# Transposing q and k of a lightning-attention block on VectorE instead of TensorE

## The chip, the cores and the metric

The kernel runs on one core of one Trainium2 chip. The metric is the device time of one execution in microseconds (us). A profiled execution gives the span from the first to the last instruction and what each engine did in it. Engines are named as in the profile: PE is TensorE, PEld its weight loads, DVE is VectorE, ACT is ScalarE, POOL is GpSimd and SP is SyncE, which only issues transfers here.

## The reference

Two blocks, one behind the other. The first is lightning attention with a decay per head, over B, H, S, D = 4, 8, 768, 64:

```python
for b in range(nb):                       # blocks of 64 positions
    intra = einsum('bhic,bhjc->bhij', qb, kb) * Dmask
    intra = einsum('bhij,bhjd->bhid', intra, vb)
    inter = einsum('bhid,bhde->bhie', qb * lam_pow, kv_state)
    out[:, :, sl] = intra + inter
    kv_state = lam_block * kv_state + einsum('bhsd,bhse->bhde', kb * rev_pow, vb)
```

Its output, laid out as x of 3072 tokens by 512 features, goes through `h = x @ w_in; g = h - tanh(h); out = g @ w_out`, with w_in 512 x 2048 and w_out 2048 x 512. Everything is float32 at the output; the weights arrive as 64-bit floats and are rounded on the chip.

## The kernel before, in words

The sequence is cut into NG = 6 groups of BLK = 128 positions. A group holds one **chunk** per batch element b, so there are 24 chunks (g, b), each with all 8 heads; heads go in NP = 4 pairs, since two heads of 64 features fill 128 partitions. One group of 4 chunks gives 512 tokens, one pass of the dense block.

`load` (L116) issues three transfers a chunk on SP's queue, one each for q, k and v. Each puts 128 positions on the partitions and 8 heads x 64 features behind them (256 KB in packets of 256 bytes). Their buffers come from rings: 2 for q, 3 for k, 4 for v. A load waits until the last reader of its buffer is done, and the loads behind it on the queue wait with it.

`att_transpose` (L227) needs q and k with features on the partitions. PE transposes each pair of heads (L234) into a PSUM bank, `tq` or `tk`; ACT copies the banks to `qt` and `kt` in SBUF (L237, L238; two buffers each); DVE makes `qd`, q times the powers of the decay, from `tq` (L242, not in the first group), and multiplies `k_nat` in place by the decay to the end of the block (L245, not in the last group). `att_scores` (L248) multiplies `kt` by `qt` on PE and masks on DVE (L259). `att_out` joins the masked scores times v with `qd` times the running state (L296, L302); ACT brings the result to SBUF as `xt` (L306). `att_state` forms k times v (L271) and adds it to the state on DVE (L275, L276). `att_sums` forms sums of blocks of x (L312 to L315).

The dense block of the first group is plain (`up_plain` L437, `down_plain` L454) while weights arrive and are rounded. From the second group on both products are done with seven block products in place of eight (`up` L366, `down` L408): an up stage for each of four u, then a down stage, with products in the order 1, 2, 6, 5, 7, 4, 3. They use PSUM banks y (two), z and w (one each), which ACT and DVE clear (L342 to L355, L376, L377, L383, L384, L412, L414). The weights of the down products, `wb`, 1 MB each, are loaded on POOL's queue into two buffers (L395).

Attention of group g+1 is woven into the dense block of group g by hand, in pieces: the first two chunks' transposes after u=1, their scores after u=2, their output and state after down product 2; the other two chunks' transposes after product 6, their scores after 5, and the rest after 7:

```python
for n, more in ((2, p0[2:]), (6, p1[0:1]), (5, p1[1:2]), (7, p1[2:])):
    down(g, n)
    run(more)
```

Beyond that, the order on each engine and all waits are set by the framework when the kernel is built.

Of the kernel before, what the change touches and what calls it, by code (L numbers as in the profile page):

```python
# [9 lines left out]
F32 = mybir.dt.float32  # L10
# [3 lines left out]
AF = mybir.ActivationFunctionType  # L14
AL = mybir.AluOpType

BLK = 128
# [5 lines left out]
def kernel(  # L23
# [31 lines left out]
    nc = tc.nc  # L55
    B, H, S, D = q.shape
    NTOK, DM = out.shape
    DFF = moe_w_in.shape[1]
    NP = H // 2
    KI = DM // 128  # L60
    KO = DFF // 128
    NG = S // BLK
# [10 lines left out]
    io = ctx.enter_context(tc.tile_pool(name="io", bufs=4))  # L73
# [9 lines left out]
    ident = const.tile([128, 128], F32)  # L83
# [5 lines left out]
    for j in range(2):  # L89
        for p in range(NP):  # L90
            h = 2 * p + j
# [3 lines left out]
    fwd = const.tile([128, NP, BLK], F32)  # L95
# [16 lines left out]
    raw = {}  # L112
# [2 lines left out]

    def load(n):  # L116

        while at["loaded"] < min(n, len(chunks)):
            g, b = chunks[at["loaded"]]
            t = []  # L120
            for name, src, bufs in (("q", q, 2), ("k", k, 3), ("v", v, 4)):
                x = io.tile([128, H, D], F32, name=f"{name}_nat", tag=name, bufs=bufs)
                nc.sync.dma_start(out=x, in_=src[b, :, ts(g, BLK), :].rearrange("h s d -> s h d"))
                t.append(x)
            raw[g, b] = t
            at["loaded"] += 1

# [66 lines left out]
    def round_block(w, raw64):  # L194
# [18 lines left out]
        nc.vector.tensor_tensor(wi, wi, r, op=AL.add)  # L213

    load(2)
    load_weights(WAHEAD)

# [3 lines left out]
    def bank(name, tag, bufs):  # L221
        return psum.tile([128, 512], F32, name=name, tag=tag, bufs=bufs)


    tr, sc, kdec, xt = {}, {}, {}, {}

    def att_transpose(g, bs):  # L227
        for b in bs:
            load(g * B + b + 1)
            qn, kn, _ = raw[g, b]  # L230
            tq, tk = (bank(n, "att", 4).rearrange("d (p s) -> d p s", p=NP) for n in ("tq", "tk"))
            for t, x in ((tq, qn), (tk, kn)):
                for p in range(NP):
                    nc.tensor.transpose(out=t[:, p, :], in_=x[:, 2 * p:2 * p + 2, :], identity=ident)  # L234
            qt = work.tile([128, NP, BLK], F32, name="qt", tag="qt")
            kt = work.tile([128, NP, BLK], F32, name="kt", tag="kt")
            nc.scalar.activation(qt, tq, AF.Copy)  # L237
            nc.scalar.activation(kt, tk, AF.Copy)  # L238
            qd = None
            if g > 0:  # L240
                qd = work.tile([128, NP, BLK], F32, name="qd", tag="qd")
                nc.vector.tensor_tensor(qd, tq, fwd, op=AL.mult)  # L242
            if g < NG - 1:
                kp = kn.rearrange("s (p j) d -> s p j d", j=2)
                nc.vector.tensor_tensor(kp, kp, bwd, op=AL.mult)  # L245
            tr[g, b] = (qt, kt, qd)

# [14 lines left out]
    def att_state(g, bs):  # L262
        if g == NG - 1:
            return

        kv = bank("kv", "att", 4).rearrange("d (b p e) -> d b p e", b=2, p=NP)
        for n, b in enumerate(bs):
            _, kd, vn = raw[g, b]
            for p in range(NP):
                for j in range(2):  # L270
                    nc.tensor.matmul(out=kv[ts(j, 64), n, p, :], lhsT=kd[:, 2 * p + j, :], rhs=vn[:, 2 * p + j, :],  # L271
                                     start=n == 0 and p == 0, stop=True, skip_group_check=True)
        st = state[:, bs[0]:bs[0] + 2]
        if g > 0:
            nc.vector.tensor_tensor(st, st, lam_blk, op=AL.mult)  # L275
            nc.vector.tensor_tensor(st, st, kv, op=AL.add)  # L276
        else:
            nc.vector.tensor_copy(st, kv)

    def att_out(g, bs):  # L280
        half = bs[0] // 2
        xt[g, half] = xpool.tile([128, KI, HB], F32, name=f"xt{half}", tag=f"xt{half}")

        ops = [bank("op", "att", 4).rearrange("d (p b s) -> d p b s", p=2, b=2) for _ in range(2)]

        def dst(n, p, j):
            return ops[p // 2][ts(j if p < 2 else 1 - j, 64), p % 2, n, :]


        if g > 0:  # L290
            for n, b in enumerate(bs):
                for p in (0, 1):
                    for j in range(2):
                        r = ts(j, 64)
                        for pp in (p, p + 2):
                            nc.tensor.matmul(out=dst(n, pp, j), lhsT=state[r, b, pp, :], rhs=tr[g, b][2][r, pp, :],  # L296
                                             start=n == 0 and p == 0, stop=False, skip_group_check=True)
        for n, b in enumerate(bs):
            ss, vn = sc.pop((g, b)), raw[g, b][2]
            for p in range(NP):  # L300
                for j in range(2):
                    nc.tensor.matmul(out=dst(n, p, j), lhsT=vn[:, 2 * p + j, :], rhs=ss[:, j, p, :],  # L302
                                     start=g == 0 and n == 0 and p % 2 == 0, stop=n == 1 and p % 2 == 1,
                                     skip_group_check=True)
        for x in range(2):
            nc.scalar.activation(xt[g, half][:, 2 * x:2 * x + 2, :].rearrange("d p (b s) -> d p b s", b=2), ops[x], AF.Copy)  # L306
# [11 lines left out]
    def attention(g):  # L318
        pieces = [[(fn, g, bs) for fn in (att_transpose, att_scores, att_out, att_state)] for bs in ((0, 1), (2, 3))]
        pieces[1].append((att_sums, g, None))  # L320
        return pieces
# [234 lines left out]
```

## Time and profile before

| what | value |
|---|---|
| median of 3 runs | 723.77 us (722.71 to 724.51) |
| the profiled execution, whole | 722.81 us |
| its span | 721.0 us |
| granted TensorE clock | 0.988 |
| PE busy | 698.4 us (97%) |
| DVE busy | 337.4 us (47%) |
| ACT busy | 182.5 us (25%) |
| SP's queue q1 | 76,000 packets, 20.98 MB |
| chain that ended last, on PE | 89% of the span |

Busy time is the time in which at least one instruction of that engine ran. The chain is followed back from the last instruction to whatever released each step. A row of the groups of instructions names line, engine, operation, output and inputs, and gives busy time, mean duration and the idle time in front. The profiled execution took 1.8 us more than its span and 1.0 us less than the median of the runs.

### The profile page before, as it was taken

The page shows a single profiled execution, that of the slowest core. Times are in us where ns is not written, and L with a number is a line of the kernel's source. Part 1 is how long each engine was busy: PE and PEld are TensorE (multiplying, and loading weights), DVE is VectorE, ACT ScalarE, POOL GpSimd, SP SyncE. Part 2 cuts the span into 40 slices and gives each one's busy share as a digit, 9 for nine tenths or more (in the row PEclk, how much of TensorE's full clock was granted, in tenths as well). Part 3 has the DMA queues.
Part 4 walks back from the last instruction along what each step waited for, and adds up shares of the span by engine and source line. Part 5 has one row for each costly group of instructions (what it writes and reads, how often), then busy time and mean ns, then how long its engine had stood idle before and what let it go on. Part 6 is the DMA issues. An engine that isn't in the chain of part 4 may idle for free.

```text
span 721.0 us, 9989 instructions
## 1 busy us (share of the span) xinstructions
PE 698.4 (97%) x4224; PEld 585.4 (81%) x4224; DVE 337.4 (47%) x575; ACT 182.5 (25%) x312; POOL 68.1 (9%) x115
## 2 busy tenths in 40 slices
PE   6789999999999999999999999999999999999996
PEld 5568865557888888888888888888888888888885
DVE  6778956862656131564422455422345522254400
ACT  3536413423421210332200342111242111132100
POOL 0222202311000001000101000001000101100110
PEclk9799999999999999999999999999999999999998
DMA  9997708855101755011556110556310332400341
GB/s 212 237 217 222 250 3 262 266 163 170 29 1 62 216 178 159 1 30 58 160 160 171 65 30 5 167 166 172 106 45 0 113 116 93 147 1 0 132 143 76
DMA packets 89324, 86.63 MB, mean 120 GB/s; under 512 B 76864, under 2 KB 76864, under 8 KB 84800
## 3 DMA queue, kind: packets, MB, share of 16 engines
q0 software_dynamic: 13136, 65.02, 27.1%
q1 hardware_dynamic: 76000, 20.98, 14.1%
q8 instruction: 33, 0.54, 0.3%
q14 instruction: 11, 0.09, 0.0%
q10 hardware_dynamic: 144, 0.00, 0.0%
HBM read 72.36 MB, written 13.63 MB: 119 GB/s over the span
## 4 chain that ended last, share of the span: by engine, by line
PE 89%; DVE 4%; DMA 3%; ACT 2%; issue 2%; SPq 1%; POOLq 0%; POOL 0%; ACTq 0%
PE y L408 19%; PE y L366 18%; PE z L366 9%; PE z L408 9%; PE op L454 8%; PE h L437 7%; PE w L408 5%; PE w L366 4%; PE op L302 3%; DMA raw<-in_moe_w_in_dram 2%; PE sp L255 2%; DVE ss L259 2%; PE tk L234 1%; PE op L296 1%; PE tq L234 1%
## 5 line engine op out<-in xcount | busy, mean ns | idle before, releaser
L408 PE MATMUL y<-wb,g 128*128 128x256 f32 x640 | 142.3, 380 | 0.7 <-ACT o L349 0.7
L408 PEld LDWEIGHTS y<-wb,g 128*128 128x128 f32 x640 | 120.9, 190 | 18.0 <-ACT o L349 1.1
L366 PE MATMUL y<-xt,w 128*128 128x256 f32 x320 | 74.0, 382 | 1.1 <-ACT g L347 1.1
L376 ACT ACTIVATE th<-g 128x512 f32<-128x512 f32 x60 | 37.8, 630 | 141.7 <-DVE g L344 96.8
L366 PEld LDWEIGHTS y<-xt,w 128*128 128x128 f32 x320 | 60.1, 190 | 11.3 <-ACT g L347 2.7
L437 PE MATMUL h<-xt,w 128*128 128x256 f32 x256 | 61.9, 401 | 6.9 <-DVE w L213 4.7
L395 POOL DMA_DIRECT2D wb<-factors x35 | 18.9, 540 | 493.7 <-PE y L408 383.2
L437 PEld LDWEIGHTS h<-xt,w 128*128 128x128 f32 x256 | 50.6, 202 | 15.2 <-issue 3.5
L377 DVE TENSOR_TENSOR g<-g,th 128x512 f32<-128x512 f32 x60 | 41.4, 691 | 35.5 <-ACT th L376 35.5
L454 PE MATMUL op<-wt,g 128*128 128x512 f32 x128 | 56.1, 595 | 0.0
L454 PEld LDWEIGHTS op<-wt,g 128*128 128x128 f32 x128 | 24.0, 190 | 28.5 <-issue 27.7
L259 DVE TENSOR_TENSOR ss<-sp,mask 128x512 f32<-128x512 f32 x48 | 30.8, 682 | 27.3 <-PE sp L255 27.3
L350 DVE TENSOR_TENSOR g<-g,z 128x512 f32<-128x512 f32 x20 | 13.8, 688 | 57.5 <-ACT g L349 57.5
L366 PE MATMUL w<-xt,w 128*128 128x256 f32 x160 | 38.2, 382 | 0.0
L366 PE MATMUL y<-tt,ws 128*128 128x256 f32 x160 | 37.8, 379 | 0.0
L366 PE MATMUL y<-tt,w 128*128 128x256 f32 x160 | 37.8, 379 | 0.0
L366 PE MATMUL z<-xt,ws 128*128 128x256 f32 x160 | 37.8, 379 | 0.0
L366 PE MATMUL z<-tt,ws 128*128 128x256 f32 x160 | 37.8, 379 | 0.0
L408 PE MATMUL z<-wb,gs 128*128 128x256 f32 x160 | 35.4, 379 | 0.0
L408 PE MATMUL w<-wb,g 128*128 128x256 f32 x160 | 35.3, 379 | 0.0
L408 PE MATMUL z<-wb,g 128*128 128x256 f32 x160 | 35.3, 379 | 0.0
L408 PEld LDWEIGHTS w<-wb,g 128*128 128x128 f32 x160 | 30.4, 190 | 4.1
(88 smaller groups left out, 885.3 us busy)
## 6 DMA issues: line engine op xcount, KB each, us to landing
wb<-factors POOLq DMA_DIRECT2D x35, 1024.0 KB, 5.4
raw<-in_moe_w_out_dram POOLq DMA_DIRECT2D x16, 512.0 KB, 4.5
q_nat<-in_q_dram SPq DMA_DIRECT2D x24, 256.0 KB, 5.5
k_nat<-in_k_dram SPq DMA_DIRECT2D x24, 256.0 KB, 5.2
v_nat<-in_v_dram SPq DMA_DIRECT2D x24, 256.0 KB, 5.3
factors<-wt POOLq DMA_DIRECT2D x8, 768.0 KB, 5.8
out_dram<-o POOLq DMA_DIRECT2D x20, 256.0 KB, 5.4
raw<-in_moe_w_in_dram POOLq DMA_DIRECT2D x6, 512.0 KB, 7.3
```

The costliest lines, as they stand in the source:

```text
L234: nc.tensor.transpose(out=t[:, p, :], in_=x[:, 2 * p:2 * p + 2, :], identity=ident)
L255: nc.tensor.matmul(out=sp[j][:, p, :], lhsT=kt[ts(j, 64), p, :], rhs=qt[ts(j, 64), p, :], start=True, stop=True)
L259: nc.vector.tensor_tensor(ss[:, j], sp[j], mask[:, j], op=AL.mult)
L302: nc.tensor.matmul(out=dst(n, p, j), lhsT=vn[:, 2 * p + j, :], rhs=ss[:, j, p, :], start=g == 0 and n == 0 and p % 2 == 0, stop=n == 1 and ...
L350: nc.vector.tensor_tensor(dst(22), dst(22), z, op=AL.add)
L366: nc.tensor.matmul(out=t[:, m, :], lhsT=wt[:, kt, ts(m, 128)], rhs=x[:, kt, :], start=first and m == 0 and kt == 0, stop=kt == 1, skip_gro ...
L376: nc.scalar.activation(th, src, AF.Tanh)
L377: nc.vector.tensor_tensor(dst(c), src, th, op=AL.subtract)
L395: nc.gpsimd.dma_start(out=blks[key], in_=factors[XAT[FACT[key[1]][1]]])
L408: nc.tensor.matmul(out=t[:, m, :], lhsT=a, rhs=wb[:, kt, :], start=first and m == 0 and kt == 0, stop=kt == KH - 1, skip_group_check=True)
L437: nc.tensor.matmul(out=hm[:, m, :], lhsT=w1[u][:, i, a, ts(m, 128)], rhs=xt[0, t][:, i, :], start=m == 0 and i == 0, stop=i == KI - 1, ski ...
L454: nc.tensor.matmul(out=obank[b], lhsT=g, rhs=wt[:, 2 * a:2 * a + 2, :], start=kt == 0 and a == 0, stop=kt == KH - 1 and a == 1)
```

## The change

In the first group q and k are handled as before, except that the ring for q has 3 buffers and that one bank after the other is allocated. From the second group on, q and k come as blocks: for each pair of heads and each quarter of 32 partitions, one transfer brings 32 features of one head, so that position t of a run of 32 positions is on the partitions and run r and feature a lie behind. That is 16 transfers of 16 KB for q and 16 for k, in packets of 128 bytes, into tiles `q_blk` and `k_blk`. Both take their buffers from the one ring "q" of 3. One DVE transpose of 128 x 512 in blocks of 32 x 32 turns each tile into `qt` or `kt`. `qd` is made from `qt` in SBUF. The natural k is still loaded, except in the last group, since the state needs it; the natural q is not.

```diff
     def load(n):
...
-            t = []
-            for name, src, bufs in (("q", q, 2), ("k", k, 3), ("v", v, 4)):
-                x = io.tile([128, H, D], F32, name=f"{name}_nat", tag=name, bufs=bufs)
-                nc.sync.dma_start(out=x, in_=src[b, :, ts(g, BLK), :].rearrange("h s d -> s h d"))
-                t.append(x)
+            t = {}
+            for name, src, bufs in (("q", q, 3), ("k", k, 3), ("v", v, 4)):
+                if g > 0 and name in "qk":
+                    x = io.tile([128, NP, BLK // 32, 32], F32, name=f"{name}_blk", tag="q", bufs=3)
+                    for p in range(NP):
+                        for c in range(4):
+                            blk = src[b, 2 * p + c // 2, ts(g, BLK), ts(c % 2, 32)]
+                            nc.sync.dma_start(out=x[ts(c, 32), p], in_=blk.rearrange("(r t) a -> t r a", t=32))
+                    t[name + "b"] = x
+                if g == 0 or name in "kv" and (name, g) != ("k", NG - 1):
+                    x = io.tile([128, H, D], F32, name=f"{name}_nat", tag=name, bufs=bufs)
+                    nc.sync.dma_start(out=x, in_=src[b, :, ts(g, BLK), :].rearrange("h s d -> s h d"))
+                    t[name] = x
...
     def att_transpose(g, bs):
         for b in bs:
             load(g * B + b + 1)
-            qn, kn, _ = raw[g, b]
-            tq, tk = (bank(n, "att", 4).rearrange("d (p s) -> d p s", p=NP) for n in ("tq", "tk"))
-            for t, x in ((tq, qn), (tk, kn)):
-                for p in range(NP):
-                    nc.tensor.transpose(out=t[:, p, :], in_=x[:, 2 * p:2 * p + 2, :], identity=ident)
+            t = raw[g, b]
             qt = work.tile([128, NP, BLK], F32, name="qt", tag="qt")
             kt = work.tile([128, NP, BLK], F32, name="kt", tag="kt")
-            nc.scalar.activation(qt, tq, AF.Copy)
-            nc.scalar.activation(kt, tk, AF.Copy)
+            for dst, x in ((qt, "q"), (kt, "k")):
+                if g > 0:
+                    nc.vector.transpose(out=dst.rearrange("d p i -> d (p i)"), in_=t[x + "b"].rearrange("d p r a -> d (p r a)"))
+                else:
+                    tp = bank("tp", "att", 4).rearrange("d (p s) -> d p s", p=NP)
+                    for p in range(NP):
+                        nc.tensor.transpose(out=tp[:, p, :], in_=t[x][:, 2 * p:2 * p + 2, :], identity=ident)
+                    nc.scalar.activation(dst, tp, AF.Copy)
...
-                nc.vector.tensor_tensor(qd, tq, fwd, op=AL.mult)
+                nc.vector.tensor_tensor(qd, qt, fwd, op=AL.mult)
...
-                kp = kn.rearrange("s (p j) d -> s p j d", j=2)
+                kp = t["k"].rearrange("s (p j) d -> s p j d", j=2)
```

The rest of the diff only fetches the tiles of a chunk by name instead of by place.

More of the change, by code (lines that the diff above doesn't have):

```diff
@@ L267, in att_state @@
         for n, b in enumerate(bs):
-            _, kd, vn = raw[g, b]
+            kd, vn = raw[g, b]["k"], raw[g, b]["v"]
             for p in range(NP):
@@ L298, in att_out @@
         for n, b in enumerate(bs):
-            ss, vn = sc.pop((g, b)), raw[g, b][2]
+            ss, vn = sc.pop((g, b)), raw[g, b]["v"]
             for p in range(NP):
```

## The prediction

> **What bounds the kernel now.** I read the page from the top: busy time by engine, the slices, the chain that ended last, and then the chain and the timeline in the stretches that hold a transpose.
>
> ```profile
> PE 698.4 (97%) x4224; PEld 585.4 (81%) x4224; DVE 337.4 (47%) x575; ACT 182.5 (25%) x312; POOL 68.1 (9%) x115
> PE 89%; DVE 4%; DMA 3%; ACT 2%; issue 2%; SPq 1%; POOLq 0%; POOL 0%; ACTq 0%
> ```
>
> TensorE (PE) is busy 97% of the span and carries 89% of the chain; the groups of instructions show no wait of PE longer than a few us after the first 45 us. So a PE instruction taken away in the steady part should shorten the run, if what it hands on is still in time. What the transposes cost is read from the chain between 190 and 194 us, not from their mean duration, because matmuls overlap:
>
> ```profile
> 190.15 1.73 PE z L366 x8
> 191.88 0.44 PE tq L234 x4
> 192.32 0.44 PE tk L234 x4
> 192.75 0.44 PE tq L234 x4
> 193.19 0.44 PE tk L234 x4
> 193.63 1.73 PE w L366 x8
> ```
>
> Sixteen transposes (two chunks) push the next product back by 193.63 - 191.88 = 1.75 us, 109 ns each, and they lie on the chain. Twelve us later the same chain leaves PE (205.73 to 213.34, the scores of u=2): it runs through DVE L355, L377, L259, L384, L344 and ACT L376, and PE waits for it at 213.34. In that stretch DVE has no slack.
>
> DMA (packets, MB, share of 16 engines) and the queue that issues the loads:
>
> ```profile
> q1 hardware_dynamic: 76000, 20.98, 14.1%
> L123 SPq DMA_DIRECT2D q_nat<-in_q_dram x24: 367/368/2009, 0.7 to 532.8; - x24
> L123 SPq DMA_DIRECT2D k_nat<-in_k_dram x24: 367/552/3649, 1.2 to 533.3; - x24
> L123 SPq DMA_DIRECT2D v_nat<-in_v_dram x24: 576/1367/5202, 1.9 to 495.5; - x24
> ```
>
> The columns are min/median/max ns that SP spends on one issue. q1 is SP's queue: 14.1% of 16 engines over 721.0 us for 76,000 packets is 21.4 ns a packet. q issues in 368 ns; v, behind two others, in 1367, which is what 1024 packets take to drain (1024 x 21.4 / 16 = 1.37 us). So an issue has a floor of about 0.37 us and above it follows the packets queued.
>
> **What the Trainium skill says.** "VectorE: DVE Perf Modes", The three transpose paths: DVE transposes 32x32 blocks only, 311 ns for 128x128 bf16. "Vector Engine (DVE) Microarchitecture Reference", 3.8 The reshape front-end: the array sustains one element per cycle per lane. The trace has no DVE transpose; its DVE COPY of 128x512 f32 from PSUM (L424) takes 692 ns. "DMA: Bandwidth & Descriptors", Specifications: transfers want 512 B or more for line rate. The trace agrees: 256 B per 21.4 ns on 16 engines is 191 GB/s at best, and slices with large packets reach 266. The same page, Anatomy of one DMA, puts about 2 us fixed on a transfer, most of it the receipt; here the least from issue to landing is 3.0 us (q_nat) and 3.1 for the 4 KB lam_all.
>
> **The change part by part.**
>
> *Removed on PE:* 5 groups x 4 chunks x 8 = 160 transposes: 10 pairs of chunks x 1.75 = **17.4 us** off the chain (the pairs at 67.3, 130.4 and 243.4 us show the same 1.75). PE follows at once with products whose inputs are old, so nothing else becomes late there but the scores: 14.1 us after the first pair, 8.7 after the second.
>
> *Removed on ACT:* 40 copies (L237, L238) of about 0.61 = 24 us. ACT is 25% busy and they are not on the chain: credit 0.
>
> *Added on DVE:* 40 transposes of 128x512. No row shows one. Estimates from the two pages: at 0.96 GHz 512 elements stream in 0.53 us, the lower bound; 311 ns for 128 is 133 streaming and 178 fixed, so 0.71 for 512; 1.4 if four-byte elements go at half rate, the upper bound. I take 0.7, the COPY's too. Per group 8 x 0.7 = 5.6 us (11.2 at most), against 113.2 - 47.1 = 66 us of idle DVE in the steady group from 191.5 to 304.7. Cost 0 where they fall in idle time. qd (L242, 20 x 0.686) reads SBUF for PSUM and stays. bwd (L245) no longer waits for PE (25.0 us of idle before it now); that is no chain time, credit 0, between -1 and +1.
>
> *DMA work:* 24 natural loads go (24,576 packets), 640 block loads of 16 KB come (128 packets each, 81,920). Net +57,344 packets x 21.4 / 16 = +77 us of all engines over some 560 us. In a steady group the windows give about 39 us of DMA time in 113; it becomes about 55. Not a bound. The factor loads (wb, 1 MB, 5.4 us) share the engines; the tightest one that meets block loads has 10 us (243.9 to 254.1), so cost 0, at most 0.5 us a group.
>
> *SP's queue:* per steady group 128 block issues x 0.37 to 0.60 us (0.60 is what SP needs for the 256 KB weight blocks, L149) = 47 to 77 us, and 8 natural ones, 8 x about 1 to 1.4 = 8 to 11. 55 to 88 us in a period of 110: it fits. But all is in order, and a load that waits for its buffer holds those behind it.
>
> *The new wait.* q and k blocks share 3 buffers in the order q0 k0 q1 k1 ..., so k of chunk c waits for the DVE transpose of q of chunk c-1, then takes 16 x 0.37 to 0.60 = 6 to 10 us of issue and 3 us to land: 9 to 13 us. Today's q load has 50 us or more of lead. What saves it: each engine runs its instructions in an order fixed beforehand, and the trace shows it is not the code's: ready work is pulled far forward into idle DVE time. The weight sums L178 stand after the whole plain down stage in the code and run at 32 us. The transposes need only qt and kt (2 buffers), free when the scores two chunks earlier are done, so those of one pair can run 40 us before their scores. After the first pair's scores (207.7) three block tiles lie ready and only k of chunk 3 is late, landing by about 225, scores at 252. The wait that matters is then not PE's for the scores but DVE's: behind a transpose put too early stand the evictions. From 215.3 PE has a down product of 6.9 us that needs no DVE; after it the z bank is needed at 224. Bounds: 0 to 6 us of PE a group; I take 0.8 x 5 = **+4**. In the down stage (255 to 282) the same wait is covered: z has 12 us and the sums L312 to L315 over 12.
>
> *Start:* group 1's blocks load at 35 to 60 us, where DMA slices are full and weights are awaited; about 3,000 more packets x 21.4 / 16 = 4 us of DMA, part of it before 44.8, where PE stops waiting. I take **+1.5** (0 to 3).
>
> Sum against the profiled execution's own 722.81 us (span 721.0, 1.8 around it): 722.8 - 17.4 + 4 + 1.5 = 710.9. The median of the runs is 1.0 above that execution: **712 us**.
>
> **The rivals.**
>
> *DVE waits at the head of its queue (slower), 0.22.* If the order was made with block loads that cost next to nothing, DVE stands at the transpose of k in chunk 3 for up to 9 us in the up stage. The cover there is two products, 3.5 us (between z's last product and its next). PE loses 5.5 x 5 = 27, plus 3 at the start: 722.8 - 17.4 + 27 + 3 = 735, with the median 736. It decides from a lateness of 7 us (3.5 of cover and 3.5 gained a group). For it: the trace has the same mechanism once, on ACT:
>
> ```profile
> 42.52 0.66 ACT L206 ACTIVATE w<-raw 128x512 f32<-128x512 f32 x1 [2.48 <-DMA raw<-in_moe_w_in_dram]
> 44.11 1.09 ACT L306 ACTIVATE xt<-op 128x512 f32<-128x512 f32 x2
> 44.76 1.60 PE L437 MATMUL h<-xt,w 128*128 128x256 f32 x3 [2.02 <-ACT xt L306]
> ```
>
> ACT waits 2.48 us for a transfer while an eviction whose input is done stands behind it, and PE waits 2.02 us. Against: 40 us of lead, and idle DVE only where PE can spare it.
>
> *SP is the bound (slower), 0.08.* From 0.77 us an issue on (128 x 0.77 + 11 = 110). At 0.9 a group takes 126: +16 x 4 = 64, so 770. For: v's 1.37; against: that is drain of 1024 packets, an eighth of it here.
>
> *The transposes land where DVE is the chain (same), 0.13.* The second pair becomes possible just at the scores of 205.7 to 213.3. Four in that stretch are 2.8 us of the 3.5 gained a group: 722.8 - 17.4 + 14 + 1.5 = 721. Against: the evictions come earlier in the code and are served first.
>
> That the blocks are not q and k transposed can be left out: partition 32c+a of a pair is head c//2, feature 32(c%2)+a.
>
> **How the numbers follow.** Forecast 0.57, own range 705 to 718. A measurement of this kernel tells about 0.3% (2.2 us) from no change. Faster: 0.57 + 0.03 of the third rival = 0.60; same: 0.08; slower: 0.22 + 0.08 + 0.02 = 0.32. Range 704 to 742: below it 0.03 (all waits free and the start no worse), above it the SP bound and 0.06 of DVE's wait.
>
> **What would show it.** PE with 160 fewer instructions and z L366 followed by w L366 at once where tq and tk stood; a new DVE row of 40 at 0.6 to 1.4 us; SP issues of blocks near 0.4 us; DVE waits on the block DMAs of a few us each, most in down stages. Wrong, if PE's busy share drops below 95% with waits for DVE or ACT evictions at each u=2 to 3, or if scores wait for kt.

## The result, and the profile after

The changed kernel takes 744.49 us (median of 4 runs, 741.17 to 747.34) against 723.24 us before: ratio 1.0294, 95% interval 1.0242 to 1.0346. It is slower by 2.9%, and outside the range of the forecast. The profiled execution took 747.34 us, its span is 745.6 us against 721.0.

The page's busy times and chain by engine, of the kernel after:

```profile
PE 689.1 (92%) x4064; PEld 572.4 (77%) x4064; DVE 361.3 (48%) x615; ACT 162.6 (22%) x272; POOL 68.0 (9%) x115
PE 57%; DMA 19%; SPq 9%; DVE 8%; issue 4%; ACT 2%; DVEq 0%; POOLq 0%; POOL 0%; ACTq 0%
```

PE has 160 instructions fewer and is busy for 9.3 us less, yet its share fell from 97% to 92%, and the chain now runs through DMA and SP's queue for 28% of the span. Where the transposes stood, one product follows the other at once. From the chain in order of time (start, us, what):

```profile
208.35 1.73 PE z L377 x8
210.08 1.73 PE w L377 x8
```

So the time that the change was to take out did go. To see what came in, take one mark a group: PE's second down product (w), which appears in the chain as one row in both kernels. First the kernel before:

```profile
225.70 6.91 PE w L408 x32
338.91 6.91 PE w L408 x32
452.11 6.91 PE w L408 x32
565.32 6.91 PE w L408 x32
672.20 6.91 PE w L408 x32
```

and the kernel after:

```profile
242.15 6.91 PE w L419 x32
363.00 6.91 PE w L419 x32
481.89 6.91 PE w L419 x32
591.60 6.91 PE w L419 x32
696.73 6.91 PE w L419 x32
```

| stretch | before | after | difference |
|---|---|---|---|
| start to the first mark | 225.70 | 242.15 | +16.45 |
| first period | 113.21 | 120.85 | +7.64 |
| second | 113.20 | 118.89 | +5.69 |
| third | 113.21 | 109.71 | -3.50 |
| fourth (one pair of chunks) | 106.88 | 105.13 | -1.75 |
| sum | | | +24.53 |

The third period is the change as it was meant: two pairs of chunks at 1.75 us. The first two lose 11.1 and 9.2 us beside that gain, and the first stretch, in which three pairs are saved (5.25 us), loses 21.7. In its up stages the attention woven in is that of the last group: blocks come as before (a DVE transpose waits 4.22 us for one at 523.14), but no natural k is loaded.

What PE waited for, from the timeline of PE after (in brackets the idle time in front and what ended it):

```profile
152.68 0.43 PE L307 MATMUL op<-qd,state 64*64 64x128 f32 x2 [3.95 <-DVE ss L270]
194.04 3.78 PE L377 MATMUL z<-xt,ws 128*128 128x256 f32 x8 [8.73 <-DVE g L361]
309.34 6.05 PE L377 MATMUL y<-xt,w 128*128 128x256 f32 x16 [8.54 <-ACT g L358]
427.68 6.61 PE L377 MATMUL y<-xt,w 128*128 128x256 f32 x16 [6.03 <-ACT g L358]
```

Each is a wait for an eviction, that is, for ACT or DVE to take a finished product out of its PSUM bank. What held the evictions up shows in DVE's timeline in front of 309:

```profile
295.65 0.69 DVE L366 TENSOR_TENSOR o<-o,z 128x512 f32<-128x512 f32 x1 [3.62 <-PE z L419]
306.85 0.69 DVE L256 TENSOR_TENSOR k_nat<-k_nat,mask 128x512 f32<-128x512 f32 x1 [10.51 <-DMA k_nat<-in_k_dram]
307.46 0.68 DVE L355 TENSOR_TENSOR g<-g,w 128x512 f32<-128x512 f32 x1
```

DVE stood 10.51 us at L256, the multiplication of natural k by the decay. Behind it in DVE's order was L355, the eviction of w, which ACT's tanh, ACT's next eviction and then PE waited for. The same stands in front of 194 (13.84 us at L256) and 427 (8.00). And why natural k was late, from SP's timeline:

```profile
198.19 0.43 SPq L132 DMA_DIRECT2D v_nat<-in_v_dram  x1
229.18 8.74 SPq L128 DMA_DIRECT2D k_blk<-in_k_dram  x16
...
288.11 3.92 SPq L128 DMA_DIRECT2D q_blk<-in_q_dram  x8
292.13 11.38 SPq L128 DMA_DIRECT2D k_blk<-in_k_dram  x16
303.61 0.38 SPq L132 DMA_DIRECT2D k_nat<-in_k_dram  x1
```

From 198.6 to 229.2 SP issues nothing: the next k block waits for a block buffer, that is for the DVE transpose of the q before it (30.5 us in SP's waits). Then it issues almost without a pause for 75 us. The natural k that DVE wants at 296 is issued at 303.61, right behind 16 blocks that took 11.38 us, and lands 3.22 us later.

The waits also cost PE its clock. Windows around the wait, the granted clock (1.00 is full speed) in the column before the last two (DMA share and GB/s):

```profile
300.00:303.00 3.00, 0.80 (x4) 0.37 (x2) 0.00 (x0) 0.00 (x0) 0.00 (x0) 1.00 0.83 257
304.50:309.00 4.50, 0.00 (x0) 0.00 (x0) 1.45 (x3) 0.82 (x2) 0.00 (x0) 0.50 0.70 141
309.00:313.50 4.50, 4.16 (x10) 3.35 (x11) 0.53 (x1) 0.63 (x2) 0.00 (x0) 0.50 0.20 32
315.00:330.00 15.00, 15.00 (x71) 13.21 (x70) 6.70 (x11) 5.50 (x10) 0.00 (x0) 1.00 0.06 13
```

The clock is halved during the wait and stays so for some 5 us after it. In the chain the three products from 309.34 take 7.78 us where they take 5.18 elsewhere (324.03 us): 2.6 on top of a wait of 8.54, together the 11.1 that the period lost. After the wait of 6.03 it is 8.33 for 5.18: 9.2 in all.

### The profile page after: what moved, and what is told of

The parts are those of the page before. It is cut to its first block, busy times and chain, and to the rows that moved or that the text cites. A ratio compares the mean times of both kernels' runs of the same rounds, so it can differ in the third digit from the quotient of the medians.

```text
span 745.6 us, 10434 instructions
## 1 busy us (share of the span) xinstructions
PE 689.1 (92%) x4064; PEld 572.4 (77%) x4064; DVE 361.3 (48%) x615; ACT 162.6 (22%) x272; POOL 68.0 (9%) x115
## 2 busy tenths in 40 slices
DMA packets 156530, 90.90 MB, mean 122 GB/s; under 512 B 144064, under 2 KB 144064, under 8 KB 152000
## 3 DMA queue, kind: packets, MB, share of 16 engines
q1 hardware_dynamic: 143200, 25.21, 18.8%
## 4 chain that ended last, share of the span: by engine, by line
PE 57%; DMA 19%; SPq 9%; DVE 8%; issue 4%; ACT 2%; DVEq 0%; POOLq 0%; POOL 0%; ACTq 0%
PE y L377 16%; PE y L419 15%; SPq L128 8%; PE z L377 8%; DMA q_blk<-in_q_dram 6%; PE z L419 6%; PE w L419 5%; DMA k_blk<-in_k_dram 5%; DMA k_nat<-in_k_dram 3%; PE w L377 3%; DMA raw<-in_moe_w_in_dram 3%; DMA v_nat<-in_v_dram 2%; DVE ss L270 2%; PE op L313 2%; PE sp L266 1%
## 5 line engine op out<-in xcount | busy, mean ns | idle before, releaser
L377 PE MATMUL y<-xt,w 128*128 128x256 f32 x320 | 79.4, 402 | 15.6 <-ACT g L358 15.6
L377 PEld LDWEIGHTS y<-xt,w 128*128 128x128 f32 x320 | 63.7, 202 | 28.1 <-ACT g L358 18.0
L448 PE MATMUL h<-xt,w 128*128 128x256 f32 x256 | 58.7, 387 | 6.4 <-DVE w L222 6.2
L448 PEld LDWEIGHTS h<-xt,w 128*128 128x128 f32 x256 | 48.8, 194 | 13.7 <-issue 4.8
L256 DVE TENSOR_TENSOR k_nat<-k_nat,mask 128x512 f32<-128x512 f32 x20 | 13.8, 691 | 75.3 <-DMA k_nat<-in_k_dram 72.5
L377 PE MATMUL z<-xt,ws 128*128 128x256 f32 x160 | 39.7, 393 | 8.7 <-DVE g L361 8.7
L377 PEld LDWEIGHTS z<-xt,ws 128*128 128x128 f32 x160 | 31.4, 197 | 13.6 <-DVE g L361 9.1
```

The lines of the kernel that those rows point to most:

```text
L377: nc.tensor.matmul(out=t[:, m, :], lhsT=wt[:, kt, ts(m, 128)], rhs=x[:, kt, :], start=first and m == 0 and kt == 0, stop=kt == 1, skip_gro ...
L448: nc.tensor.matmul(out=hm[:, m, :], lhsT=w1[u][:, i, a, ts(m, 128)], rhs=xt[0, t][:, i, :], start=m == 0 and i == 0, stop=i == KI - 1, ski ...
```

## The experiments

Theory A after the result: DVE stands at L256 for a natural k that comes late on SP's queue, and the evictions behind it keep PE waiting. Theory B: the blocks and their packets themselves slow the run. Ratios are to the kernel before on the same chip, whose median was 721.6 to 722.9 us.

| run | median us | ratio (95% interval) |
|---|---|---|
| e1_no_bwd | 708.96 | 0.982 (0.979 to 0.985) |
| e2_nat_pool | 709.38 | 0.9821 (0.9798 to 0.9845) |
| e3_nat_first | 713.24 | 0.9874 (0.9844 to 0.9904) |
| e4_q_only | 715.47 | 0.9893 (0.9862 to 0.9925) |
| e5_ring8 | 719.16 | 0.9955 (0.9937 to 0.9973) |
| e6_bwd_late | 744.90 | 1.0308 (1.0254 to 1.0362) |
| e7_pool_ring8 | 718.57 | 0.994 (0.9923 to 0.9958) |
| e8_pool_from3 | 708.02 | 0.979 (0.9763 to 0.9818) |
| e9_from3 | 738.96 | 1.0237 (1.0212 to 1.0261) |
| e10_k_pool | 707.27 | 0.9795 (0.978 to 0.981) |

**e1_no_bwd.** It leaves out the multiplication at which DVE stood, from the second group on, so that the state lacks this decay.

```diff
-            if g < NG - 1:
+            if g == 0:
                 kp = t["k"].rearrange("s (p j) d -> s p j d", j=2)
                 nc.vector.tensor_tensor(kp, kp, bwd, op=AL.mult)
```

> Leaves out the multiplication of natural k by the decay (L256) from the second group on; all loads stay. Theory A (DVE stands at L256 for a natural k that comes late on SP's queue, behind the blocks, and the evictions stand behind it): the DVE waits of 72.5 us on k_nat go, the periods of the two slow groups fall from 120.9 and 118.9 us to 109.7, the PE waits of 8.7, 8.5 and 6.0 us and the clock dips after them go too; 707 to 716 us. Theory B (the blocks themselves are late, or the load on DMA and SP slows the run): the transposes keep their waits of 29 us and the time stays over 735.

Measured 708.96 us, with every load still made. The first three periods are 109.71, 109.71 and 109.99 us. The transposes keep their waits for blocks (39.6 us in all on DVE, 29.4 before this edit), so these cost nothing in those periods. Theory B falls. The first stretch still loses 4.3 us (first mark at 224.72, against 225.70 less 5.25). PE's instructions stand in the same order as in the changed kernel, but those on DVE shifted, so this run alone does not show that the place of L256 was the cause.

**e2_nat_pool and e10_k_pool.** The natural loads are issued from POOL's queue; in e10 the condition reads `g > 0 and name == "k"`, so that only k's are.

```diff
-                    nc.sync.dma_start(out=x, in_=src[b, :, ts(g, BLK), :].rearrange("h s d -> s h d"))
+                    (nc.gpsimd if g > 0 else nc.sync).dma_start(out=x, in_=src[b, :, ts(g, BLK), :].rearrange("h s d -> s h d"))
```

> Natural k and v from the second group on are issued on POOL's queue, not behind the blocks on SP's. Theory A: natural k is there before DVE needs it, the waits of L256 go, 708 to 718 us; a natural load that waits for its buffer on POOL's queue can hold a factor load behind it, up to 2 us a group. Theory B: still over 735, since blocks and DMA work are the same.

> Only natural k goes to POOL's queue; natural v stays on SP behind the blocks. Theory A (the wait of L256 for natural k is the one that costs): as with k and v on POOL, 706 to 713 us. If v, which PE needs for the output and the state, is held up as well and counts: 715 to 730 us.

Measured 709.38 and 707.27 us. In both kernels PE's instructions stand in the same order as in the changed kernel; what differs is the queue of the moved loads and the order on DVE, ACT and POOL. From e10's list of DVE's waits, and from its timeline:

```profile
DVE k_nat L256 <- DMA k_nat<-in_k_dram: 18.8, 5, 5.4
```

```profile
266.95 1.28 DVE L256 TENSOR_TENSOR k_nat<-k_nat,mask 128x512 f32<-128x512 f32 x2
268.33 0.69 DVE L435 COPY o<-y 128x512 f32<-128x512 f32 x1
275.23 0.69 DVE L366 TENSOR_TENSOR o<-o,z 128x512 f32<-128x512 f32 x1 [6.22 <-PE z L419]
277.03 0.69 DVE L355 TENSOR_TENSOR g<-g,w 128x512 f32<-128x512 f32 x1 [1.11 <-PE w L377]
```

18.8 us for natural k in place of 72.5, the longest 5.4 in place of 13.8, and no wait of PE over 1.2 us after 44 us. On DVE the second of the two multiplications stands two evictions earlier than in the changed kernel, ahead of L435 and L366, and starts there without a wait: the load itself is early, and not only its reader moved. 90.90 MB and 640 block loads are moved as before the edit. With v left on SP nothing is lost, so k was the load that mattered. This is Theory A shown by its cause, and a version that is about 2% faster than the kernel before.

**e3_nat_first.** Natural k and v of a chunk ahead of its blocks on SP.

```diff
             for name, src, bufs in (("q", q, 3), ("k", k, 3), ("v", v, 4)):
+                if g == 0 or name in "kv" and (name, g) != ("k", NG - 1):
...
+            for name, src, bufs in (("q", q, 3), ("k", k, 3), ("v", v, 4)):
                 if g > 0 and name in "qk":
...
-                if g == 0 or name in "kv" and (name, g) != ("k", NG - 1):
```

> Natural k and v of a chunk stand ahead of its blocks on SP's queue. Theory A: L256's waits become short, but the ring of 3 for natural k makes the fourth chunk's natural k wait for the state of the first two (L282), and its blocks with it, so that the second pair's transposes come late: some of the gain is given back, 712 to 735 us. Theory B: over 735.

Measured 713.24 us, near the good end. DVE still waits 41.8 us for natural k, longest 9.18, but it takes up the work behind these waits before PE needs it: the first three periods are 109.71, 109.71 and 109.98 us. POOL's queue is thus not what the repair needs. From DVE's timeline:

```profile
245.59 0.69 DVE L257 TENSOR_TENSOR k_nat<-k_nat,mask 128x512 f32<-128x512 f32 x1 [9.18 <-DMA k_nat<-in_k_dram]
...
279.41 0.69 DVE L257 TENSOR_TENSOR k_nat<-k_nat,mask 128x512 f32<-128x512 f32 x1 [4.40 <-DMA k_nat<-in_k_dram]
...
281.21 0.68 DVE L356 TENSOR_TENSOR g<-g,w 128x512 f32<-128x512 f32 x1
```

A wait of 9.18 us costs nothing here; one of 8.00 cost 9.2 us at 425 us in the changed kernel. Length is not what decides. DVE's first eviction of the up stage (L355, here L356) starts 55.3 us after the mark in e2, e5 and e10. In the changed kernel the natural k ahead of it is in at 64.7 and 62.2 us after the mark; here its multiplication starts at 54.5 us, and in e10 at 45.8.

**e4_q_only.** k goes the old way.

```diff
-                if g > 0 and name in "qk":
+                if g > 0 and name == "q":
...
-                if g == 0 or name in "kv" and (name, g) != ("k", NG - 1):
+                if g == 0 or name in "kv":
...
-                if g > 0:
+                if g > 0 and x == "q":
                     nc.vector.transpose(
```

> Only q goes by blocks and DVE; k is loaded as before and transposed on PE and copied by ACT. PE keeps 80 transposes (8.7 us). Theory A: a ring of 3 for q alone gives SP three chunks of lead and half as many block loads, natural k is hardly late: 714 to 720 us. Theory B: half of the loss stays, about 730.

Measured 715.47 us. The periods are 111.46 us: 1.75 saved in each of the first three, half of the full change, and DVE waits for no block. In these periods half of the blocks gave half of the gain and none of the loss. The first stretch gained nothing (225.78 against 225.70), where 2.6 us were saved; PE waits 2.84 us at 97.59 for L453 there.

**e5_ring8 and e7_pool_ring8.** More room for blocks from the third group on; e7 with the natural loads on POOL as well.

```diff
-                    x = io.tile([128, NP, BLK // 32, 32], F32, name=f"{name}_blk", tag="q", bufs=3)
+                    if g == 1:
+                        x = io.tile([128, NP, BLK // 32, 32], F32, name=f"{name}_blk", tag="q", bufs=3)
+                    else:
+                        if name == "q":
+                            both = stage.tile([128, 2, NP, BLK // 32, 32], F32, name="both", tag="raw64", bufs=WAHEAD)
+                        x = both[:, "qk".index(name)]
```

> From the third group on, q and k blocks of a chunk lie in one of four 4 KB buffers that the weights' staging no longer needs (room for 8 block tiles in place of 3); the loads stay on SP in the same order. Theory R (natural k is late because SP stands up to 37 us for a block buffer, with natural k behind it, and then has 50 us of issues to catch up): SP runs ahead, L256 has no wait in the steady groups, their periods fall to 109.7 us; the first stage keeps its waits; 715 to 726 us. Theory I (SP's issues of some 0.5 us each are too slow in themselves): the slow groups stay near 119 to 121 us, about 742.

> Natural loads on POOL's queue and the larger ring together. If the two repairs act on one wait, they do not add: within 2 us of the version with POOL's queue alone, 706 to 711 us; if the blocks' own waits on DVE (27 us there) cost anything, 703 to 706.

e5 measured 719.16 us and all three full periods are 109.71 us, as theory R said. SP's waits for the transposes fell from 138.0 to 29.2 us, with the same number of issues, so the ring held SP up and not the price of an issue. Against my expectation, L256 (L261 in e5) was not freed of waits: it waits 36.7 us in all. It is over in time, as DVE's timeline shows:

```profile
280.11 0.69 DVE L261 TENSOR_TENSOR k_nat<-k_nat,mask 128x512 f32<-128x512 f32 x1 [8.03 <-DMA k_nat<-in_k_dram]
...
287.05 0.69 DVE L360 TENSOR_TENSOR g<-g,w 128x512 f32<-128x512 f32 x1 [1.11 <-PE w L382]
```

It starts 7 us ahead of DVE's first eviction of the up stage. e7 was expected at 711 at most and took 718.57. The larger ring begins in buffers that the weights still use in the plain stage (SP waits 26.6 us for raw<-in_moe_w_out_dram). Its first transposes wait 9.65 and 7.32 us for their blocks; behind the second stands the eviction of w (L360), and PE waits 8.24 us at 183 us. In e5 it is 5.89 us on DVE and 6.08 of PE at 177. The repairs do not add; this one brings a wait of its own. It is also the rival of the prediction to the letter, a block's transpose in front of an eviction: either reader of a late load costs there.

**e6_bwd_late.** L256 moved in the code to the products that need it.

```diff
     def att_transpose(g, bs):
...
-            if g < NG - 1:
-                kp = t["k"].rearrange("s (p j) d -> s p j d", j=2)
-                nc.vector.tensor_tensor(kp, kp, bwd, op=AL.mult)
...
     def att_state(g, bs):
...
+        for n, b in enumerate(bs):
+            kp = raw[g, b]["k"].rearrange("s (p j) d -> s p j d", j=2)
+            nc.vector.tensor_tensor(kp, kp, bwd, op=AL.mult)
```

> The multiplication L256 stands in att_state, just ahead of the products that need it, in place of att_transpose; loads, buffers and SP's order are those of the changed kernel. Theory A (only its place on DVE hurts, ahead of evictions): natural k comes as late as before, but hardly anything stands behind a wait for it; periods near 110 us, 707 to 716 us. If the lateness of natural k itself counted (state products late on PE), 735 or more.

Measured 744.90 us: nothing gained, against my expectation. DVE's timeline says why:

```profile
307.00 0.69 DVE L277 TENSOR_TENSOR k_nat<-k_nat,mask 128x512 f32<-128x512 f32 x1 [9.30 <-DMA k_nat<-in_k_dram]
307.61 0.68 DVE L355 TENSOR_TENSOR g<-g,w 128x512 f32<-128x512 f32 x1
```

The instruction (L277 now) stands in front of L355 as before. Its place in the code did not set its place on DVE, so the run does not test what it was made for. What it does show is that the same order with the same late load gives the same loss.

**e8_pool_from3 and e9_from3.** The change from the third group on, with the natural loads on POOL or on SP.

```diff
-                if g > 0 and name in "qk":
+                if g > 1 and name in "qk":
...
-                if g == 0 or name in "kv" and (name, g) != ("k", NG - 1):
+                if g < 2 or name in "kv" and (name, g) != ("k", NG - 1):
...
-                if g > 0:
+                if g > 1:
                     nc.vector.transpose(
```

> Blocks, DVE transposes and POOL's queue for the natural loads start with the third group; the second is transposed on PE as the first. PE keeps 32 transposes (3.5 us) and loses the DVE waits of the plain stage (5.3 us of PE in the version with POOL's queue from the second group on, 2.0 in the kernel before): 705 to 709 us.

> The change from the third group on, all loads on SP as in the changed kernel: the second group is transposed on PE. If the loss has two separate parts, the plain stage's 21.7 us goes, the two slow groups keep their 11.1 and 9.2 us, and PE saves 14.0 us: 722 - 14 + 20 = 728 us (724 to 732). If the slow groups are an echo of a late first stage (SP never catches up), they come clean and it is 706 to 712 us.

e8 measured 708.02 us, as expected: between 46 and 680 us PE has no wait over 0.3 us. It gives up 3.5 us of saving and has none of the plain stage's waits; e2 and e10 keep the saving and some waits. No interval tells e8 from e10. e9 was expected at 728 and took 738.96. Its plain stage is clean, but PE has three long waits and not two:

```profile
186.29 3.78 PE L377 MATMUL z<-xt,ws 128*128 128x256 f32 x8 [9.78 <-DVE g L361]
299.88 6.01 PE L377 MATMUL y<-xt,w 128*128 128x256 f32 x16 [6.03 <-ACT g L358]
419.01 1.22 PE L377 MATMUL y<-xt,w 128*128 128x256 f32 x2 [6.85 <-ACT g L358]
```

The wait at 186 is the 8.73 us of the changed kernel at 194: it belongs to the third group's natural k (14.88 us of DVE at L256), not to the second group's blocks. So there are three such places, one at the first up stage. That is about the 11 us between 728 and 739.

## Why the prediction was wrong

**Right by its working.** PE gained 3.50 us a full group, as worked out. The DVE transpose takes 0.697 us (0.7 taken). A block issue takes SP 0.430 us at the median and 0.485 in the mean, within 0.37 to 0.60 (the least is 0.311). Blocks land in 2.5 to 3.0 us. SP's queue is not too slow for the work: e5 has the same issues and full-speed periods.

**The step that failed** is the line on L245 in what is added on DVE: "bwd (L245) no longer waits for PE ... credit 0, between -1 and +1". With the transposes gone nothing held that instruction back on PE's side, and it was pulled ahead to wait for a transfer instead, 72.5 us in all, and PE stood with it for 8.73, 8.54 and 6.03 us. The prediction had seen that "ready work is pulled far forward", and counted on it for the transposes alone. I followed the new wait from the block's buffer to the block's transpose, and wrote that a load that waits "holds those behind it", but did not ask which loads those were. Natural k was one, and its reader stood on DVE in front of the up stage's evictions. The waits of the transposes themselves, for which I took +4, cost nothing measurable in the full groups of e1, where they stayed.

**The rival that came true in part** is DVE waiting at the head of its queue. Its mechanism was right: in front of the evictions of an up stage DVE stood 8 to 14 us, over the 7 us named, and PE lost its time there. The instruction was another, and it happened at three places and not at five. That its 736 us lies near the 744.49 measured is in part luck: it has 27 us for five groups, where three places took some 31, and 3 for the start, where the plain stage lost some 10.9. The rival of transposes in a stretch where DVE is the chain did not come: the third period has the whole gain.

**Mis-sized terms.** The start was taken at +1.5 for weights delayed by block loads before 44.8 us; PE was not late there (it starts at 42.96, ahead of the 44.76 of before). What the first stretch lost, 21.7 us, is some 10.8 at 194 us (8.73 and a product 2.05 longer) and some 10.9 in the plain stage, of which 4.7 us of wait follow a stand of DVE at L256 at 146.8 us, and 4.65 us at 95 to 103 are waits for L453 on a DVE that is full there. The waits for L453 do not need L256: without it, in e1, 3.26 us of them stay. In e8 and e9, where PE transposes the second group, there are none, but in e3, which has that group's blocks, there are none over 0.3 us either. What makes them stays open. No case held the clock: about 2 to 3 us after each of three long waits, 7.8 in all. DMA work was taken at +77 us of all engines; by the line of q1, it is half:

```profile
q1 hardware_dynamic: 143200, 25.21, 18.8%
```

18.8% of 745.6 less 14.1% of 721.0 is 38.5 us, 15.7 ns a packet over the queue in place of 21.4. Two terms were off. The 128-byte packets were priced at the queue's mean. And the packets grew by 67,200, not by 57,344: in the packet records of both traces every transfer on q1 has 16 packets of 4 bytes as well, and there are 616 transfers more.

## What to carry to other kernels

When a load that has to wait for a buffer is put on an in-order queue, list every load behind it and the engine on which each one's reader stands; the price is paid by what stands behind that reader. A wait in an engine's order costs by where it ends against the next eviction, not by its length: 9.18 us was free and 8.00 us cost 9.2. Where a kernel's instructions are reordered for it, moving a line in the code may move nothing; moving the load to another queue did.

## What the runs showed of the hardware

After PE had waited 8.5 us, the granted clock was 0.50, as in the windows above, and three products took 7.78 us in place of 5.18; after 6.0 us they took 8.33. At half speed the 2.60 and 3.15 us lost are 5.2 and 6.3 us of work. The Trainium skill, "TensorE: Matmul & The Clock Gate", Why this matters for your kernels, warns of idle gaps over about 3 us. The trace agrees: the clock was also at 0.50 after the waits of 8.73 us (193.5 to 197.5 us) and 3.95 us (154 to 157 us), and at 1.00 after those of 1.20 to 1.83 us at 95 to 103. I had not priced it.

Packets of 128 bytes take less time than those of 256, but more than half of it. In the packet records of the trace after, on q1, a packet of 128 bytes takes 12.7 ns in the mean, one of 256 bytes 19.8 (20.2 before) and one of 4 bytes 9.3. "DMA: Bandwidth & Descriptors", Why small descriptors are slow, gives a packet a fixed part and a part by bytes: 3 cycles and one for every 32 bytes. By that count 128 bytes are 7 cycles and 256 are 11, an estimate of 0.64 from the page; 12.7 / 19.8 is 0.64 too.
